# Layer normalisation of the first four tiles: tile 1's mean and variance by two ScalarE passes, doubled columns by GpSimd, V's parts and copies in another order

## The chip, the cores and the metric

The kernel runs on one core of a Trainium2 chip. The metric is the device time of one execution in microseconds. Engines are named as in the profile: PE is TensorE (matmuls; PEld its weight loads), DVE is VectorE, ACT is ScalarE, POOL is GpSimd, SP is SyncE, which here only issues transfers.

## The reference

The input x has 2048 rows of 576 columns in bfloat16. It is normalised without weights, and an attention over a sliding window and a gated feed-forward layer run side by side on the result:

```python
def _layernorm(x, axis=-1, eps=1e-5):
    m = jnp.mean(x, axis=axis, keepdims=True)
    v = jnp.var(x, axis=axis, keepdims=True)
    return (x - m) / jnp.sqrt(v + eps)
...
    xn = _layernorm(x, axis=-1)
    return x + _A_ref(xn, A_wqkv, A_wo) + _B_ref(xn, B_w1, B_w3, B_w2)
```

`_A_ref` projects xn to q, k and v (32 heads of 18 columns), lets each row see itself and the 255 rows before it, applies softmax and multiplies by wo. `_B_ref` computes (silu(xn @ w1) * (xn @ w3)) @ w2 with 4608 inner columns.

## The kernel before

The 2048 rows go in four chunks of 512, each of four tiles of 128 rows. For each chunk there are projections (line 439), 36 units of the feed-forward layer's first products (L675) with the attention's scores, exponentials and products dealt in between (L559, L568, L616), and then the sums of the second products and the output (L741, L760). Nearly all of it is TensorE's work, and the matmuls use half of the array's rows each (`tile_position`), so two run side by side.

Everything is recorded by `add(engine, ...)` in the order of the Python code. Each engine executes its own instructions strictly in that order; `_Prog.resolve` works out from the buffers' keys (r = reads, w = writes a new version, j = joins the writers of the present one) which semaphores an instruction has to wait for. So where a call stands in the code decides what it is queued behind.

The change is in the prologue, before the first chunk's projections. There the four tiles of chunk 0 are normalised and turned. (The tiles of the later chunks go another way, through a transposing DMA in `xn_send`.) For each tile t with buffers i = t % 2:

- `load_x` brings the tile into `xp`; tile 0 on SP's queue, tiles 1 to 3 on ScalarE's.
- `ln_stats` computes mean and variance on VectorE: a statistics instruction for each half of the columns (L355, L357), an aggregation into `mv` (L358). Then 1e-5 is added into `vpe` (L359, on VectorE for tiles 0 and 3, on GpSimd for 1 and 2), and GpSimd raises that to the power -0.5 into `rstd` (L361).
- `ln_apply` writes `xn` = (x - mean) * rstd on VectorE (L367). The row of `xn` is 640 wide: 576 columns, and then the last 64 once more, so that the fifth block of 128 holds columns 512 to 575 twice. It is done in two instructions, of 576 and of 64 columns.
- `xn_turn` transposes `xn` on TensorE by ten small matmuls with the identity into two banks of PSUM (L379), five blocks by two halves of the rows, and copies them to `xnT` (L390): for tiles 0 to 2 two ScalarE copies, for tile 3 one ScalarE and one VectorE copy. The banks are `SC` = (6, 7) for tiles 0 and 2 and `JOBS[1]` = (2, 3) for tiles 1 and 3.

V's projection (`proj_part` with kind "v") has ten matmuls in part 0 and eight in part 1 for each tile. `proj_begin` records part 0 of a new product and then part 1 of the one still open; `proj_end` records only that part 1 and the copies from PSUM to `va` (`v_evac`, L488 on ScalarE and L490 on VectorE, two instructions each). For tiles 0 and 1 these copies are held in the lists `moves` and `late` and recorded after the loop. V's tile 2 uses the banks `SC` again. `warm` issues matmuls on zeros.

Meanwhile GpSimd clears buffers and, when Q's and K's weights have landed, deals them into `wp` with nine copies (L851, `deal`); Q's and K's projections need them. SP issues the loads of x, V's weights and Q's and K's weights, then the first six parts of w13 (L315, behind tile 1's `xnT`), then the two copies `xn_swap` that fill `xnS` from `xnT` with the halves of the partitions exchanged (L404). In `unit_pairs` matmuls n = 4 to 7 read `xnS`, the others `xnT`.

Of the kernel before, what the change touches and what calls it, by code (L numbers as in the profile page):

```python
# [5 lines left out]
dt = mybir.dt  # L6
ACT = mybir.ActivationFunctionType
# [157 lines left out]
def bass_parallel_sum__sliding_block__glu_gated_swiglu__prompt_kernel(  # L165
# [13 lines left out]
    Dh = D // H  # L179
# [18 lines left out]
    with ExitStack() as es:  # L198
# [121 lines left out]
        def load_w13(behind=(), parts=6):  # L320
            for _ in range(parts):
                load_part((), behind)
# [26 lines left out]
                w=[("w2", s)], after=after, dma=f"w2_{s}")  # L349


        def ln_stats(t, s, part):
            i = t % 2
            if part == 0:
                add("dve", lambda e: e.bn_stats(stats[i][:, 0, :], xp[s][:, 0:HD]), r=[("xp", s)], w=[("stats", i)])  # L355
                return
            add("dve", lambda e: e.bn_stats(stats[i][:, 1, :], xp[s][:, HD:D]), r=[("xp", s)], j=[("stats", i)])  # L357
            add("dve", lambda e: e.bn_aggr(mv[i][:], stats[i][:]), r=[("stats", i)], w=[("mv", i)])  # L358
            add("dve" if t in (0, TB - 1) else "pool", lambda e: e.tensor_scalar(vpe[i][:], mv[i][:, 1:2], 1e-5, None, op0=ALU.add),  # L359
                r=[("mv", i)], w=[("vpe", i)])  # L360
            add("pool", lambda e: e.tensor_tensor(rstd[i][:], vpe[i][:], neghalf[:], ALU.pow),  # L361
                r=[("vpe", i), "neghalf"], w=[("rstd", i)])

        def ln_apply(t, s):
            i = t % 2
            for n, (c0, c1) in enumerate(((0, D), (512, D))):
                add("dve", lambda e, n=n, c0=c0, c1=c1: e.tensor_scalar(  # L367
                    xn[i][:, c0 + 64 * n:c1 + 64 * n], xp[s][:, c0:c1], mv[i][:, 0:1], rstd[i][:, 0:1],
                    op0=ALU.subtract, op1=ALU.mult),
                    r=[("xp", s), ("mv", i), ("rstd", i)], **{"j" if n else "w": [("xn", i)]})  # L370

        def xn_turn(t, banks, eng="dve"):
            i = t % 2
            c, tt = divmod(t, TB)
            for k in range(5):
                for r in range(2):
                    r0 = 64 * r
                    bv = half_bank(banks[r])[:, 64 * k:64 * k + 64]
                    add("pe", lambda e, bv=bv, r0=r0, k=k: e.transpose(  # L379
                        bv, xn[i][r0:r0 + 64, k * 128:(k + 1) * 128], ident[r0:r0 + 64, r0:r0 + 64],  # L380
                        tile_position=(r0, 0)),
                        r=[("xn", i), "ident"], **{"j" if k else "w": [("ps", banks[r])]})
            both = PS[:, banks[0]:banks[0] + 2, :].bitcast(dt.bfloat16)
            src = both[:, :, 0:320].rearrange("p r (k f) -> p k r f", f=64)
            dst = xnT[:, c % 2, :, tt * 128:(tt + 1) * 128].rearrange("p k (r f) -> p k r f", f=64)
            for n, (k0, k1) in enumerate(((0, 2), (2, 5))):
                d, s = dst[:, k0:k1, :, :], src[:, k0:k1, :, :]
                if eng[1] == "dve":
                    d, s = dst[:, :, n, :], src[:, :, n, :]
                move = (lambda e, d=d, s=s: e.tensor_copy(d, s)) if eng[n] == "dve" else (lambda e, d=d, s=s: e.activation(d, s, ACT.Copy))  # L390
                add(eng[n], move, r=[("ps", b) for b in banks],
                    **({"j": [("xnT", c % 2, tt)]} if n else {"w": [("xnT", c % 2, tt), ("xnTa", tt)]}))

        def xn_send(t):
            i = t % 2
            c, tt = divmod(t, TB)
            add("sp", lambda e: e.dma_start_transpose(
                xnT[:, c % 2, :, tt * 128:(tt + 1) * 128], xn[i][:]),
                r=[("xn", i)], w=[("xnT", c % 2, tt)], dma=f"xnT{tt}")

        def xn_swap(c, eng):
            for n in range(2):
# [5 lines left out]
        def xk(c):  # L408
            return [("xnT", c % 2, tt) for tt in range(TB)]
# [36 lines left out]
        def proj_out(c, what, banks, later=None, late=None):  # L446
            kind, i = what
            b = banks[0]
            if kind == "q":
                t0, t1 = pair_of(c, i)  # L450
                add("dve", lambda e: e.tensor_copy(stage[:, t0, :], PS[:, b, :]), r=[("ps", b)], w=st_keys(t0))
                add("act", lambda e: e.activation(stage[:, t1, :], PS[:, b + 1, :], ACT.Copy),  # L452
                    r=[("ps", b + 1)], w=st_keys(t1))
            elif kind == "8":
                add("dve", lambda e: e.tensor_copy(
                    stage[:, i, :].rearrange("p (b f) -> p b f", b=2), PS[:, b:b + 2, 0:CH // 2]),
                    r=[("ps", b), ("ps", b + 1)], w=st_keys(i))
            else:
                for r, (eng, held) in enumerate((("act", late), ("dve", later))):
                    move = lambda r=r, eng=eng: v_evac(c, i, b, r, eng)  # L460
                    move() if held is None else held.append(move)

        COST = {"q": 1.0, "8": 0.5, "v": 0.5625}
        PROJ = [("q", 0), ("q", 1), ("v", 0), ("q", 2), ("v", 1), ("q", 3), ("v", 2), ("8", 7), ("v", 3)]
# [9 lines left out]
        def proj_begin(c, what, banks=None):  # L474
            banks = banks or job()
            last = proj_part(c, what, banks, 0)
            got = proj_end()
            pend.append((c, what, banks, last))
            return got

        def v_evac(c, tt, b, r, eng):
            pos = (c * NB + 2 * tt + r) % NV
            for p in range(2):
                src = PS[64 * r:64 * r + 64, b:b + 2, 0:HD].rearrange("p b (n e d) -> p e b n d", e=2, d=Dh)[:, p, :, :, :]
                dst = va[64 * p:64 * p + 64, pos, :, :, 0:Dh].rearrange("p (b g) n d -> p b (g n) d", b=2)
                kw = {"j" if p else "w": [("va", pos)]}
                if eng == "act":
                    add("act", lambda e, dst=dst, src=src: e.activation(dst, src, ACT.Copy), r=[("ps", b), ("ps", b + 1)], **kw)  # L488
                else:
                    add("dve", lambda e, dst=dst, src=src: e.tensor_copy(dst, src), r=[("ps", b), ("ps", b + 1)], **kw)  # L490

        def keys_of(a, b, p0, n, p):
            return kv[p0:p0 + n, a:b, :, KB * p:KB * p + KB].rearrange("q g b f -> q (g b) f")
# [172 lines left out]
        def unit_pairs(c, u, n0, n1, b0):  # L666

            fc, fl = divmod(u, 4)
            sl, wt = w13_at(c * NFC + fc)
            for n in range(n0, n1):  # L670
                for r in range(2):
                    r0 = 64 * r
                    k = 8 if n == 8 else (2 * n + r if n < 4 else 2 * (n - 4) + 1 - r)
                    src = xnT[r0:r0 + 64, c % 2, k // 2, :] if n in (0, 1, 2, 3, 8) else xnS[r0:r0 + 64, n - 4, :]
                    op = add("pe", lambda e, n=n, r0=r0, r=r, k=k, src=src: e.matmul(  # L675
                        PS[:, b0 + r, :], wt[r0:r0 + 64, k, fl * 128:(fl + 1) * 128], src,
                        start=(n == 0), stop=(n == 8), tile_position=(r0, 0)),
                        r=[("w13", sl), "xnS"] + xk(c), **{"j" if n else "w": [("ps", b0 + r)]})
            return op

        def unit_tanh(u, b0):
# [111 lines left out]
        def warm(b, n):  # L793
            for k in range(n):
                add("pe", lambda e: e.matmul(PS[:, b, :], oq[:, 0:128], oq[:], start=True, stop=True),
                    r=["oq0"], **{"j" if k else "w": [("ps", b)]})
# [17 lines left out]
        def clear_keys(a, b, behind=()):  # L814
            add("pool", lambda e: e.memset(kv[:, a:b, :, :].bitcast(dt.float32), 0.0),
                r=list(behind), w=[("k", g) for g in range(a, b)])

        clear_keys(0, 2)
        for p in range(2):
            ln_stats(0, xslot[0], p)  # L820
        moves, late = [], []
        for i in range(TB):
            if i + 1 < TB:
                for p in range(2):
                    ln_stats(i + 1, xslot[i + 1], p)
            ln_apply(i, xslot[i])
            xn_turn(i, JOBS[1] if i % 2 else SC, ("act", "dve" if i + 1 == TB else "act"))
            if i == 0:
                warm(3, 1)
                proj_begin(0, ("v", 0))  # L830
            elif i == 1:
                load_w13([("xnT", 0, 1)])
                proj_end(moves, late)
                proj_begin(0, ("v", 1))
            elif i == 2:
                proj_end(moves, late)
        for move in moves + late:
            move()
        xn_swap(0, ("sp", "sp"))
        proj_begin(0, ("v", 2), SC)  # L840
        proj_begin(0, ("v", 3))
        wf = wa[:, :, :].bitcast(dt.float32).rearrange("p k (n g c) -> p k n g c", n=2, c=2 * Dh)
        wpf = wp[:, :, :, :].bitcast(dt.float32)
# [268 lines left out]
```

## Time and profile before

| what | value |
| --- | --- |
| median of 3 runs | 559.09 us (559.08 to 559.09) |
| the profiled execution's own time | 559.1 us |
| its span, first to last instruction | 557.4 us |
| granted TensorE clock | 1.00 |
| TensorE busy | 552.2 us, 99% of the span |
| VectorE, ScalarE, GpSimd busy | 56%, 45%, 29% |
| TensorE busy in 0 to 5 us / 5 to 10 us / 10 to 15 us | 3.76 / 3.77 / 4.93 us |

A row of the timeline gives start and length in us, engine, line, operation, what it writes and reads, shapes and how many instructions are drawn together; in brackets stands how long the engine was idle before it and what ended that. The chain that ended last is followed back from the last instruction to what released each. The end of a matmul in the trace is modelled, so that the starts are the better marks of its pace.

### The profile page before, as it was taken

What the parts mean: (1) busy time and instruction counts of PE and PEld (TensorE: products, weight loads), DVE (VectorE), ACT (ScalarE), POOL (GpSimd) and SP (SyncE); (2) the same over time, 40 slices, a digit from 0 to 9 for tenths busy, and PEclk for the clock granted to TensorE, in tenths of its full rate; (3) what the DMA queues carried; (4) which work ended last, traced back from release to release, by engine and by line L of the source; (5) the groups of instructions that cost most, each with busy time, mean ns of one, the idle gap of its engine ahead of it and who ended that gap; (6) DMA issues with size and microseconds to landing.
All of it is one profiled execution on the core that took longest, in us unless ns stands there. A gap on an engine that the chain in (4) does not pass through costs nothing.

```text
span 557.4 us, 18205 instructions
## 1 busy us (share of the span) xinstructions
PE 552.2 (99%) x8012; PEld 345.5 (62%) x8012; DVE 311.0 (56%) x586; ACT 252.9 (45%) x352; POOL 163.1 (29%) x384
## 2 busy tenths in 40 slices
PE   8999999999999999999999999999999999999998
PEld 4445455677687455477766545547777664555776
DVE  8566798710365778851056668884105567767211
ACT  4357776100287776600037777650005676676000
POOL 6413454400033445330003344533000333433000
PEclk9999999999999999999999999999999999999999
DMA  9998889777556657656846746566683674651650
GB/s 251 205 195 181 192 205 220 134 181 189 139 135 140 147 135 165 153 146 181 199 110 139 171 110 171 125 162 165 162 196 87 139 171 123 151 135 28 167 151 22
DMA packets 127893, 86.07 MB, mean 154 GB/s; under 512 B 35430, under 2 KB 125502, under 8 KB 127814
## 3 DMA queue, kind: packets, MB, share of 16 engines
q1 hardware_dynamic: 88994, 62.88, 48.8%
q10 hardware_dynamic: 38820, 22.02, 15.8%
q8 instruction: 63, 1.03, 0.9%
q14 instruction: 16, 0.13, 0.1%
HBM read 71.37 MB, written 2.36 MB: 132 GB/s over the span
## 4 chain that ended last, share of the span: by engine, by line
PE 98%; DVE 1%; DMA 0%; POOL 0%; issue 0%
PE ps L675 50%; PE ps L741 29%; PE ps L439 9%; PE ps L559 6%; PE ps L616 4%; DMA xp<-in_A_x_dram 0%; DVE xn L367 0%; DVE stats L355 0%; DVE stats L357 0%; DVE mv L358 0%; POOL rstd L361 0%; DVE ofin L760 0%; DVE vpe L359 0%; PE ps L379 0%
## 5 line engine op out<-in xcount | busy, mean ns | idle before, releaser
L675 PE MATMUL ps<-xnT,w 64*128 64x512 bf16 x1400 | 182.1, 376 | 0.0
L675 PE MATMUL ps<-xnS,w 64*128 64x512 bf16 x1120 | 155.1, 376 | 0.0
L741 PE MATMUL ps<-w,hT 64*128 64x288 bf16 x2288 | 143.7, 283 | 0.0
L690 DVE SCALAR_TENSOR_TENSOR gs<-th,ps 128x512 bf16<-128x512 bf16 x144 | 97.9, 680 | 80.3 <-ACT th L684 79.5
L568 ACT ACTIVATE pt<-ps 128x1024 bf16<-128x1024 f32 (+1 forms) x112 | 113.1, 1010 | 64.0 <-PE ps L559 62.9
L741 PEld LDWEIGHTS ps<-w,hT 64*128 64x128 bf16 x2288 | 111.7, 94 | 29.6 <-issue 0.4
L675 PEld LDWEIGHTS ps<-xnT,w 64*128 64x128 bf16 x1400 | 72.9, 94 | 55.9
L595 POOL TENSOR_TENSOR pt<-pt,mk 128x128 int32<-128x128 int32 (+1 forms) x199 | 80.3, 425 | 79.5 <-ACT pt L568 79.5
L693 DVE SCALAR_TENSOR_TENSOR hT<-gs,ps 128x512 bf16<-128x512 bf16 x144 | 98.9, 687 | 5.0
L684 ACT ACTIVATE th<-ps 128x512 bf16<-128x512 f32 x144 | 85.4, 593 | 23.5 <-PE ps L675 23.3
L675 PEld LDWEIGHTS ps<-xnS,w 64*128 64x128 bf16 x1120 | 59.4, 94 | 50.8
L760 DVE TENSOR_TENSOR ofin<-ps,xp 128x288 bf16<-128x288 f32 x32 | 12.7, 452 | 125.8 <-PE ps L741 125.8
L452 ACT ACTIVATE stage<-ps 128x512 bf16<-128x512 f32 x16 | 9.6, 597 | 143.6 <-PE ps L439 141.3
L595 POOL TENSOR_TENSOR hT<-hT,mk 128x128 int32<-128x128 int32 (+1 forms) x31 | 12.4, 420 | 170.5 <-ACT hT L568 170.5
L559 PE MATMUL ps<-qv,kv 64*128 64x320 bf16 (+4 forms) x528 | 53.6, 260 | 0.0
L559 PEld LDWEIGHTS ps<-qv,kv 64*128 64x128 bf16 x528 | 28.1, 94 | 24.9 <-ACT pt L568 0.5
L439 PE MATMUL ps<-xnT,wp 64*128 64x512 bf16 (+1 forms) x360 | 39.0, 355 | 0.0
L568 ACT ACTIVATE stage<-ps 128x1024 bf16<-128x1024 f32 x24 | 24.6, 1023 | 12.6 <-PE ps L559 12.6
L638 DVE STREAM_TRANSPOSE od<-oq 128x256 bf16<-128x256 bf16 x64 | 25.8, 428 | 6.3 <-POOL oq L631 6.3
L439 PEld LDWEIGHTS ps<-xnT,wp 64*128 64x128 bf16 x360 | 20.1, 94 | 13.0
L439 PE MATMUL ps<-wv,xnT 64*128 64x288 bf16 x288 | 22.0, 283 | 0.2 <-ACT xnT L390 0.2
L595 POOL TENSOR_TENSOR stage<-stage,mk 128x128 int32<-128x128 int32 (+1 forms) x42 | 17.0, 422 | 17.3 <-ACT stage L568 17.2
(59 smaller groups left out, 334.8 us busy)
## 6 DMA issues: line engine op xcount, KB each, us to landing
w<-in_B_w_dram SPq DMA_DIRECT2D x210, 192.0 KB, 4.1
w<-in_B_w_dram ACTq DMA_DIRECT2D x70, 288.0 KB, 3.6
xp<-in_A_x_dram SPq DMA_DIRECT2D x29, 144.0 KB, 3.4
out_dram<-ofin SPq DMA_DIRECT2D x32, 72.0 KB, 3.1
xnS<-xnT SPq DMA_DIRECT2D x8, 256.0 KB, 5.1
oT<-od SPq DMA_DIRECT2D x56, 36.0 KB
pt<-in_A_wqkv_dram SPq DMA_DIRECT2D x4, 288.0 KB, 5.6
hT<-in_B_w_dram SPq DMA_DIRECT2D x6, 192.0 KB, 7.4
```

The lines of the kernel that those rows point to most:

```text
L439: op = add("pe", lambda e, out_=out_, st=st, mv=mv, n=n, r0=r0, first=first: e.matmul(out_, st, mv, start=first, stop=(part == 1 and n == ...
L559: add("pe", lambda e, r0=r0, out_=out_, kb=kb, q0=q0, nb=nb: e.matmul(out_, kb4[r0:r0 + 64, g, kb + NV - NB, :] if kb < 0 else kv[r0:r0 + ...
L568: add("act", lambda e: e.activation(pt_slot(sl)[:, 0:w, :], PS[:, SC[0]:SC[1] + 1, 0:w].rearrange("p r q -> p q r"), ACT.Exp, scale=scale) ...
L595: add("pool", lambda e, vb=vb, mm=mm: e.tensor_tensor(vb, vb, mm, ALU.mult), r=(key if n == 0 else []) + ["mk"], **{"w" if n == 0 else "j" ...
L616: add("pe", lambda e, p=p, q=q, pr=pr, sl=sl, g=g, pos=pos, q0=q0, nb=nb, col=col, first=first, n=n: e.matmul(PS[32 * q:32 * q + VW, banks ...
L638: add("dve", lambda e: e.transpose(od[i][:, g % 2, c0:c0 + CH // 2], oq[:, c0:c0 + CH // 2]), r=["oq", "oq0"], **{"j" if half or g % 2 els ...
L675: op = add("pe", lambda e, n=n, r0=r0, r=r, k=k, src=src: e.matmul(PS[:, b0 + r, :], wt[r0:r0 + 64, k, fl * 128:(fl + 1) * 128], src, star ...
L684: add("act", lambda e: e.activation(th[i][:], PS[:, bg, :], ACT.Tanh, scale=0.5), r=[("ps", bg)], w=[("th", i)])
L690: add("dve", lambda e: e.scalar_tensor_tensor(out=gs[i][:], in0=th[i][:], scalar=1.0, in1=PS[:, bg, :], op0=ALU.add, op1=ALU.mult), r=[("t ...
L693: add("dve", lambda e: e.scalar_tensor_tensor(out=hT[:, u, :], in0=gs[i][:], scalar=0.5, in1=PS[:, bu, :], op0=ALU.mult, op1=ALU.mult), r= ...
L741: op = add("pe", lambda e: e.matmul(PS[:, bank, 0:HD], stat, move, start=new, stop=False, skip_group_check=True, **tile), r=keys, after=he ...
L760: add("dve", lambda e: e.tensor_tensor(ofin[:, o, :], PS[:, bank, 0:HD], xp[xs[n]][:, d0:d0 + HD], ALU.add), r=[("ps", bank), ("xp", xs[n] ...
```

## The change

- Tile 1's mean and variance come from ScalarE (`ln_stats_act`): one pass over the tile copies it scaled by -1/(576*24) and sums the row into `vpe`, which is minus the mean over 24; a second pass squares x/24 plus that and sums the row into `mv`, which is the variance. What they write besides is left in a part of `hT` that is free at that time. GpSimd multiplies `vpe` by -24 to get the mean, adds 1e-5 and takes the power. Before, VectorE's three instructions and GpSimd's addition and power did this.
- The addition of 1e-5 and the power are taken out into `ln_root`. In the prologue the addition is on VectorE for tiles 0, 2 and 3 (tile 2's was on GpSimd), and the power is recorded where the order now wants it.
- For tiles 0 to 3 `ln_apply` writes columns 0 to 511 on VectorE and the doubled block of 128 columns on GpSimd in one instruction that reads the 64 columns twice. The doubled block has a key of its own, `xnd`, and only the last two of the ten transposes wait for it.
- The prologue's loop is written out by hand. VectorE's statistics of tile 2 begin before tile 0 is applied. On TensorE part 0 of V's tile 2 moves ahead of tile 3's turn, and part 1 of it directly behind that turn.
- The copies of V are recorded one instruction at a time. The first ScalarE and the first VectorE copy of tile 0 are recorded between tile 3's transposes and the copies from PSUM of that turn.
- In `unit_pairs` only the matmuls n = 4 to 7 wait for `xnS`, and only the others for `xnT`.

TensorE's order up to the first projection of Q was: turn 0, V0 part 0, turn 1, V0 part 1, V1 part 0, turn 2, V1 part 1, turn 3, V2 part 0, V3 part 0, V2 part 1. It becomes: turn 0, V0 part 0, turn 1, V0 part 1, V1 part 0, turn 2, V1 part 1, V2 part 0, turn 3, V2 part 1, V3 part 0.

```diff
+        def ln_root(t, eng=None):
+            i = t % 2
+            if eng is not None:
+                add(eng, lambda e: e.tensor_scalar(vpe[i][:], mv[i][:, 1:2], 1e-5, None, op0=ALU.add),
+                    r=[("mv", i)], w=[("vpe", i)])
+                return
+            add("pool", lambda e: e.tensor_tensor(rstd[i][:], vpe[i][:], neghalf[:], ALU.pow),
+                r=[("vpe", i), "neghalf"], w=[("rstd", i)])
+
+        def ln_stats_act(t, s):
+            i = t % 2
+            junk = hT[:, 0:3, :].rearrange("p t c -> p (t c)").bitcast(dt.float32)[:, 0:D]
+            keys = [("h", n) for n in range(3)]
+            root = float(D) ** 0.5
+            add("act", lambda e: e.activation(junk, xp[s][:], ACT.Copy, scale=-1.0 / (D * root), accum_out=vpe[i][:]),
+                r=[("xp", s)], w=[("vpe", i), *keys])
+            add("act", lambda e: e.activation(junk, xp[s][:], ACT.Square, bias=vpe[i][:], scale=1.0 / root, accum_out=mv[i][:, 1:2]),
+                r=[("xp", s), ("vpe", i)], w=[("mv", i), *keys])
+            add("pool", lambda e: e.tensor_scalar(mv[i][:, 0:1], vpe[i][:], -root, None, op0=ALU.mult),
+                r=[("vpe", i)], j=[("mv", i)])
+            ln_root(t, "pool")
+            ln_root(t)
...
         def ln_apply(t, s):
             i = t % 2
-            for n, (c0, c1) in enumerate(((0, D), (512, D))):
-                add("dve", lambda e, n=n, c0=c0, c1=c1: e.tensor_scalar(
-                    xn[i][:, c0 + 64 * n:c1 + 64 * n], xp[s][:, c0:c1], mv[i][:, 0:1], rstd[i][:, 0:1],
-                    op0=ALU.subtract, op1=ALU.mult),
-                    r=[("xp", s), ("mv", i), ("rstd", i)], **{"j" if n else "w": [("xn", i)]})
+            parts = [("dve", 0, 512, 0), ("pool", 512, D, 1)] if t < TB else [("dve", 0, D, 0), ("dve", 512, D, 2)]
+            for eng, c0, c1, n in parts:
+                src = xp[s][:, c0:c1]
+                if n == 1:
+                    dst, src = xn[i][:, 512:640].rearrange("p (a c) -> p a c", a=2), src.unsqueeze(1).to_broadcast([128, 2, 64])
+                else:
+                    dst = xn[i][:, c0 + 32 * n:c1 + 32 * n]
+                add(eng, lambda e, dst=dst, src=src: e.tensor_scalar(
+                    dst, src, mv[i][:, 0:1], rstd[i][:, 0:1], op0=ALU.subtract, op1=ALU.mult),
+                    r=[("xp", s), ("mv", i), ("rstd", i)], w=[("xnd", i) if n else ("xn", i)])
...
-                        r=[("xn", i), "ident"], **{"j" if k else "w": [("ps", banks[r])]})
+                        r=[("xn" if k < 4 else "xnd", i), "ident"], **{"j" if k else "w": [("ps", banks[r])]})
+            for what in between:
+                what()
...
-                        r=[("w13", sl), "xnS"] + xk(c), **{"j" if n else "w": [("ps", b0 + r)]})
+                        r=[("w13", sl)] + (["xnS"] if 4 <= n < 8 else xk(c)), **{"j" if n else "w": [("ps", b0 + r)]})
...
+        moves, late = [], []
         for p in range(2):
             ln_stats(0, xslot[0], p)
-        moves, late = [], []
-        for i in range(TB):
-            if i + 1 < TB:
-                for p in range(2):
-                    ln_stats(i + 1, xslot[i + 1], p)
-            ln_apply(i, xslot[i])
-            xn_turn(i, JOBS[1] if i % 2 else SC, ("act", "dve" if i + 1 == TB else "act"))
-            if i == 0:
-                warm(3, 1)
-                proj_begin(0, ("v", 0))
-            elif i == 1:
-                load_w13([("xnT", 0, 1)])
-                proj_end(moves, late)
-                proj_begin(0, ("v", 1))
-            elif i == 2:
-                proj_end(moves, late)
+        ln_root(0, "dve")
+        ln_root(0)
+        ln_stats(2, xslot[2], 0)
+        ln_apply(0, xslot[0])
+        ln_stats_act(1, xslot[1])
+        xn_turn(0, SC, ("act", "act"))
+        warm(3, 1)
+        proj_begin(0, ("v", 0))
+        ln_stats(2, xslot[2], 1)
+        ln_root(2, "dve")
+        ln_stats(3, xslot[3], 0)
+        ln_apply(1, xslot[1])
+        ln_root(2)
+        xn_turn(1, JOBS[1], ("act", "act"))
+        load_w13([("xnT", 0, 1)])
+        proj_end(moves, late)
+        proj_begin(0, ("v", 1))
+        ln_stats(3, xslot[3], 1)
+        ln_root(3, "dve")
+        ln_apply(2, xslot[2])
+        ln_root(3)
+        xn_turn(2, SC, ("act", "act"))
+        ln_apply(3, xslot[3])
+        first = [moves.pop(0), late.pop(0)]
+        proj_end(moves, late)
+        proj_begin(0, ("v", 2), SC)
+        xn_turn(3, JOBS[1], ("act", "dve"), first)
         for move in moves + late:
             move()
         xn_swap(0, ("sp", "sp"))
-        proj_begin(0, ("v", 2), SC)
+        proj_end()
         proj_begin(0, ("v", 3))
```

More of the change, by code (lines that the diff above doesn't have):

```diff
@@ L358, in ln_stats, with xn_turn @@
             add("dve", lambda e: e.bn_aggr(mv[i][:], stats[i][:]), r=[("stats", i)], w=[("mv", i)])
[L359 to L362, printed above, removed]
+            if t >= TB:
+                ln_root(t, "pool")
+                ln_root(t)
         def ln_apply(t, s):
             i = t % 2
-            for n, (c0, c1) in enumerate(((0, D), (512, D))):
-                add("dve", lambda e, n=n, c0=c0, c1=c1: e.tensor_scalar(
-                    xn[i][:, c0 + 64 * n:c1 + 64 * n], xp[s][:, c0:c1], mv[i][:, 0:1], rstd[i][:, 0:1],
-                    op0=ALU.subtract, op1=ALU.mult),
-                    r=[("xp", s), ("mv", i), ("rstd", i)], **{"j" if n else "w": [("xn", i)]})
-        def xn_turn(t, banks, eng="dve"):
+            parts = [("dve", 0, 512, 0), ("pool", 512, D, 1)] if t < TB else [("dve", 0, D, 0), ("dve", 512, D, 2)]
[8 more added lines that the diff above has]
+                    r=[("xp", s), ("mv", i), ("rstd", i)], w=[("xnd", i) if n else ("xn", i)])
+        def xn_turn(t, banks, eng, between=()):
             i = t % 2
@@ L398, in xn_send @@
                 xnT[:, c % 2, :, tt * 128:(tt + 1) * 128], xn[i][:]),
-                r=[("xn", i)], w=[("xnT", c % 2, tt)], dma=f"xnT{tt}")
+                r=[("xn", i), ("xnd", i)], w=[("xnT", c % 2, tt)], dma=f"xnT{tt}")
         def xn_swap(c, eng):
@@ L459, in proj_out @@
                 for r, (eng, held) in enumerate((("act", late), ("dve", later))):
-                    move = lambda r=r, eng=eng: v_evac(c, i, b, r, eng)
-                    move() if held is None else held.append(move)
+                    for p in range(2):
+                        move = lambda r=r, eng=eng, p=p: v_evac(c, i, b, r, eng, p)
+                        move() if held is None else held.append(move)
         COST = {"q": 1.0, "8": 0.5, "v": 0.5625}
@@ L479, in proj_begin, with v_evac @@
             return got
-        def v_evac(c, tt, b, r, eng):
+        def v_evac(c, tt, b, r, eng, p):
             pos = (c * NB + 2 * tt + r) % NV
-            for p in range(2):
[L484 to L490, printed above, removed]
+            src = PS[64 * r:64 * r + 64, b:b + 2, 0:HD].rearrange("p b (n e d) -> p e b n d", e=2, d=Dh)[:, p, :, :, :]
+            dst = va[64 * p:64 * p + 64, pos, :, :, 0:Dh].rearrange("p (b g) n d -> p b (g n) d", b=2)
+            kw = {"j" if p else "w": [("va", pos)]}
+            if eng == "act":
+                add("act", lambda e, dst=dst, src=src: e.activation(dst, src, ACT.Copy), r=[("ps", b), ("ps", b + 1)], **kw)
+            else:
+                add("dve", lambda e, dst=dst, src=src: e.tensor_copy(dst, src), r=[("ps", b), ("ps", b + 1)], **kw)
         def keys_of(a, b, p0, n, p):
@@ L818, in bass_parallel_sum__sliding_block__glu_gated_swiglu__prompt_kernel @@
         clear_keys(0, 2)
+        moves, late = [], []
         for p in range(2):
             ln_stats(0, xslot[0], p)
-        moves, late = [], []
-        for i in range(TB):
-            if i + 1 < TB:
-                for p in range(2):
-                    ln_stats(i + 1, xslot[i + 1], p)
-            ln_apply(i, xslot[i])
-            xn_turn(i, JOBS[1] if i % 2 else SC, ("act", "dve" if i + 1 == TB else "act"))
-            if i == 0:
-                warm(3, 1)
-                proj_begin(0, ("v", 0))
-            elif i == 1:
-                load_w13([("xnT", 0, 1)])
-                proj_end(moves, late)
-                proj_begin(0, ("v", 1))
-            elif i == 2:
-                proj_end(moves, late)
+        ln_root(0, "dve")
[25 more added lines that the diff above has]
+        xn_turn(3, JOBS[1], ("act", "dve"), first)
         for move in moves + late:
```

## The prediction

> **What bounds the kernel now.** I read the page first (busy shares, the chain that ended last), then the chain in order of time, then the timeline of the first 13 us, single instructions of it last.
>
> ```profile
> PE 552.2 (99%) x8012; PEld 345.5 (62%) x8012; DVE 311.0 (56%) x586; ACT 252.9 (45%) x352; POOL 163.1 (29%) x384
> ...
> PE 98%; DVE 1%; DMA 0%; POOL 0%; issue 0%
> ```
>
> ```profile
> 10.70 11.12 PE ps L439 x126
> 21.82 12.95 PE ps L675 x120
> ```
>
> TensorE is the bound, and from 10.70 us on it never waits for data: 126 projection matmuls run into the first units. Listing the starts of all later matmuls, I find no distance over 0.31 us after 12 us. So the end of the span moves one for one with the moment at which TensorE enters its gapless stretch. I take as marker the first projection of Q, "Q0" (the ten matmuls of 512 columns at 12.41). Only what comes before it can be won or lost.
>
> ```profile
> 4.85 0.55 POOL L361 TENSOR_TENSOR rstd<-vpe,neghalf 128x1 f32<-128x1 f32 x1 [1.06 <-DVE vpe L359]
> ...
> 5.65 0.59 DVE L367 TENSOR_SCALAR xn<-xp,mv,rstd 128x576 bf16<-128x576 bf16 x2
> ...
> 6.30 0.32 PE L379 MATMUL ps<-ident,xn 64*128 64x64 bf16 x10 [0.98 <-DVE xn L367]
> ...
> 7.86 0.31 PE L379 MATMUL ps<-ident,xn 64*128 64x64 bf16 x10
> ...
> 9.50 0.32 PE L379 MATMUL ps<-ident,xn 64*128 64x64 bf16 x10
> ...
> 9.87 1.31 ACT L390 ACTIVATE xnT<-ps 128x256 bf16<-128x256 bf16 x3 [0.89 <-PE ps L379]
> ...
> 10.25 3.67 POOL L851 COPY wp<-pt 128x45 f32<-128x45 f32 x9 [0.61 <-DMA pt<-in_A_wqkv_dram]
> ...
> 10.38 0.32 PE L379 MATMUL ps<-ident,xn 64*128 64x64 bf16 x10
> ...
> 12.41 1.24 PE L439 MATMUL ps<-xnT,wp 64*128 64x512 bf16 x10
> ```
>
> The four L379 rows are the turns of the four tiles, T0 to T3. Between them stand V's products in halves (V0a is the first ten matmuls of tile 0, V0b the last eight). Order before: T0, V0a, T1, V0b, V1a, T2, V1b, T3, V2a, V3a, V2b, Q0. T0 waits for VectorE, which is busy with tile 1's statistics until 5.74 though rstd is there at 5.40; T2 and T3 wait for VectorE too (9.45 and 10.32, plus 0.06).
>
> **The change, step by step.** A handover costs 0.06 (VectorE to TensorE, 6.24 to 6.30), 0.04 (GpSimd to VectorE, TensorE to ScalarE), 0.08 (GpSimd to itself, 6.11 to 6.19).
>
> *T0.* VectorE loses tile 1's statistics here and does one half of tile 2's (landed 5.05, 0.45 us), to 5.53. The apply, now of 512 columns, took 0.29 behind a busy engine for 576; I take 0.28, so 5.81, and T0 starts at 5.87 instead of 6.30.
>
> *The doubled columns.* The 64 columns twice, 0.21 us of VectorE per tile, become one GpSimd tensor_scalar of 128x128, g, which no row shows. Nearest below: an affine_select of 128x128, 0.29. Above: the mask product of 128x128, two inputs, 0.42 to 0.46; far above: 128x288 products, 0.68. I take 0.42, the same tile size on the same engine. But both halves wait for the same rstd, so they meet:
>
> ```profile
> 76.19 0.91 DVE L367 TENSOR_SCALAR xn<-xp,mv,rstd 128x576 bf16<-128x576 bf16 x2
> 76.36 0.71 POOL L631 TENSOR_TENSOR oq<-ofin,rden 128x288 bf16<-128x288 f32 x1 [1.50 <-DVE rden L630]
> ```
>
> The same pair of applies that takes 0.59 in the prologue takes 0.91 here, and ends 0.04 after GpSimd's product. The other way round, the vpe addition on GpSimd at 5.82 takes 0.29 instead of 0.22 and ends 0.08 after the apply it met; so 0.14 of it lies ahead of the block. I therefore count one as standing still for the other. VectorE is released first (0.04 against 0.08): xnd0 can only work from 5.81 and ends at 5.81 + 0.42 - 0.14 = 6.09.
>
> The Trainium skill, SBUF — State Buffer, section Who interferes with whom, says that VectorE in a two-port mode, which a tensor_scalar can enter, and GpSimd take one shared port pair as an exclusive lock, so that the second blocks fully. The trace agrees (0.91 against 0.59); by that rule the sum is the one below, without it that of the first rival.
>
> *Tile 1's statistics.* ScalarE starts when its table (3.56) and tile 1 (3.68) are there. Its copies take 0.38 for 256 and 0.49 for 384 columns, so 0.80 ns a column and 0.18 fixed: 0.64 for 576, two passes and a handover to about 5.04. Accumulator and bias vector are priced by no row (from nothing to double, 6.3); they are used only by the addition at 6.38, so I count nothing. GpSimd then does, behind xnd0: mean (0.22, starting 0.06 before xnd0 ends, as the copies of L851 follow one another), addition (0.08 + 0.05 for two semaphores, as the first L851 copy shows, + 0.22), power (0.08 + 0.57): rstd1 at 6.09 - 0.06 + 0.22 + 0.13 + 0.22 + 0.65 = 7.25. Before it was there at 6.77, and VectorE took it up at 7.12. Queued behind these on GpSimd are xnd1 and rstd2; T1 waits for them.
>
> *T1.* The apply from an idle engine took 0.43; 0.04 + 0.41 gives 7.70. xnd1 stands until then and ends at 7.98. Eight transposes run from 7.76, the last pair waits to 8.04 instead of 7.88. T1 is thus worth a start at 7.92, against 7.86 before: the early T0 (V0a would be done at 7.42) is lost on GpSimd's chain.
>
> *T1 to T2.* ScalarE's two evacuations and V1a between them, 7.86 to 9.40, are unchanged: 1.55. T2 may start at 9.47; GpSimd and VectorE have tile 2 ready by then (rstd2 8.49, xnd2 9.22). Before: 9.50.
>
> *T2 to Q0, the new order* T2, V1b, V2a, T3, V2b, V3a, Q0. V2a writes the banks of T2 and so waits for both evacuations: 9.50 to 10.69 before, 1.18; before, T3 filled part of that, now only V1b (0.49) does. V2a 0.62. T3 to V3a: 0.36 to the evacuation's start, 0.44, 0.06 = 0.86, of which V2b covers some 0.7; before, V2a behind T3 hid it whole. V3a 0.61. So 1.18 + 0.62 + 0.86 + 0.61 = 3.27 against 12.41 - 9.50 = 2.91 before. Q0 at 9.47 + 3.27 = 12.74: **0.33 later**.
>
> *At nothing.* V0's first pieces ahead of T3's evacuation (VectorE 0.46, ScalarE 0.40): apply 3 is done near 10.18, so they end by 10.7, before that evacuation at 11.6; without this cover up to 0.46. V0's second pieces now stand behind it and end near 12.47; Q0 needs their banks, cover 0.27. GpSimd's deals (L851) start when xnd3 is done, 10.46 instead of 10.25; Q0 needs three of them, 1.0 us, so 11.46. SP's first w13 load waits for T1's evacuation (0.06 later); the xnS copies behind its six issues wait at 13.1 as before, landed by 20.85, first needed at 22.52. That unit_pairs no longer waits for xnS in its outer matmuls takes away a wait that had ended by the 21.65 at which unit 0 starts. The later chunks keep instructions and order.
>
> **Sum.** Profiled execution: 559.10 (span 557.4, 1.7 around it); median 559.09, the same. 559.09 + 0.33 = 559.4. In general the block makes it 0.33 + 2(g - 0.42), since g enters at xnd0 and at xnd1. About what a measurement of this kernel can tell from no change is 0.2%, 1.12 us, so this is within it.
>
> **Rivals.**
> 1. *No block, a short g.* xnd0 5.90, rstd1 7.06, T1 7.57: 0.35 earlier than above, so -0.02; with g at 0.29, -0.15; 558.9 to 559.1. V0a's end at 7.42 is the floor, -0.17. For it: the meetings above are with longer GpSimd products. Against it: 0.91 against 0.59.
> 2. *GpSimd becomes the bound: slower.* g with two scalar vectors per partition could cost far more than a product; chain xnd0, mean, addition, power, xnd1 stands ahead of T1. It decides (over 0.2%) from g = 0.82 on; at 1.0 it gives +1.49, 560.6. For: one-element pow takes 0.57, a one-element addition 0.22, so GpSimd's cost hangs on the kind of operation. Against: selects, copies and products of this size lie at 0.29 to 0.46.
> 3. *ScalarE's passes come late.* They decide from 1.3 us a pass on; at 1.9 they end at 7.6 and rstd1 comes 1.2 later: near 560.6. Against: every ScalarE row is linear in columns, and no second table load is in the program.
>
> To win more than 0.2%, Q0 would have to start at 11.29; T1 at its floor gives 12.24.
>
> **Numbers.** Forecast 0.50 (its own range 559.2 to 559.7, g from 0.35 to 0.55); rival 1 0.30; rival 2 0.09; rival 3 0.03; what I don't see 0.05 within 0.2% and 0.03 faster. Faster 0.03, same 0.85, slower 0.12. The range goes from rival 1's floor, 558.9, to g = 0.69 with a power that meets an apply (0.69 instead of 0.57, as at 8.95): +0.87 + 0.12, 560.1.
>
> **What would show it.** T0 near 5.9; the GpSimd tensor_scalar at 0.42 or its end 0.28 behind the apply's; rstd1 near 7.25; T1's last pair late; two gaps on TensorE, before V2a (0.5) and V3a (0.15); Q0 at 12.7. Wrong if Q0 starts before 12.2 or after 13.5, or if TensorE waits later than Q0.

## The result, and the profile after

The changed kernel takes 560.25 us (median; 560.00 to 561.87), the kernel before 559.14 us in the same comparison. The ratio is 1.002, 95% interval 1.0012 to 1.0027: slower by 1.1 us, and outside the forecast range (558.9 to 560.1). The profiled execution took 560.29 us with a span of 558.6 us, against 559.10 and 557.4.

The page of the changed kernel, TensorE's busy time and the engines of the chain that ended last; then that chain in order of time (start and length in us):

```profile
PE 553.0 (99%) x8012; PEld 345.4 (62%) x8012; DVE 309.7 (55%) x580; ACT 254.5 (46%) x356; POOL 166.4 (30%) x388
...
PE 98%; POOL 1%; DMA 0%; DVE 0%; issue 0%; ACT 0%; POOLq 0%
```

```profile
5.47 0.94 POOL xn L395
7.88 0.96 POOL xn L395
...
12.46 10.56 PE ps L468 x116
23.02 12.95 PE ps L704 x120
```

The 1% that was VectorE's is now GpSimd's: two of its doubled blocks, 0.94 and 0.96 us long, stand in the chain itself, with its small instructions between them. The timeline shows how they got there (L395 is the apply, on DVE and on POOL; L358 the power; L406 the transposes; L468 the projections):

```profile
5.47 0.94 POOL L395 TENSOR_SCALAR xn<-xp,mv,rstd 128x128 bf16<-128x128 bf16 x1
5.49 0.46 DVE L378 BATCH_NORM_STATS2 stats<-xp 128x6 f32<-128x288 bf16 x1 [0.77 <-DMA xp<-in_A_x_dram]
5.87 0.40 DVE L395 TENSOR_SCALAR xn<-xp,mv,rstd 128x512 bf16<-128x512 bf16 x1
...
6.33 0.34 PE L406 MATMUL ps<-ident,xn 64*128 64x64 bf16 x10 [0.63 <-DVE xn L395]
6.49 0.25 POOL L370 TENSOR_SCALAR mv<-vpe 128x1 f32<-128x1 f32 x1
...
7.20 0.57 POOL L358 TENSOR_TENSOR rstd<-vpe,neghalf 128x1 f32<-128x1 f32 x1
...
7.81 0.41 DVE L395 TENSOR_SCALAR xn<-xp,mv,rstd 128x512 bf16<-128x512 bf16 x1 [0.37 <-POOL rstd L358]
7.88 0.95 POOL L395 TENSOR_SCALAR xn<-xp,mv,rstd 128x128 bf16<-128x128 bf16 x1
...
8.88 0.20 PE L406 MATMUL ps<-ident,xn 64*128 64x64 bf16 x2 [0.32 <-POOL xn L395]
...
10.33 0.34 PE L406 MATMUL ps<-ident,xn 64*128 64x64 bf16 x10
...
13.62 1.24 PE L468 MATMUL ps<-xnT,wp 64*128 64x512 bf16 x10
```

Tile 1's power in the kernel before, in the same view:

```profile
6.19 0.57 POOL L361 TENSOR_TENSOR rstd<-vpe,neghalf 128x1 f32<-128x1 f32 x1
```

Tile 0's block keeps GpSimd until 6.41. Only then come tile 1's mean (6.49), addition (6.90) and power (7.20, done at 7.77, where before rstd of tile 1 was there at 6.77). Then tile 1's own block runs to 8.83, and T1's last pair starts at 8.88; before, all of T1 was issued by 7.98. Q0 starts at 13.62 instead of 12.41, 1.21 us later, and the span has grown by 1.2. Nothing is won or lost after Q0.

### The profile page after: what moved, and what is told of

Its sections match the earlier page's. It is cut to its first block, busy times and chain, and to the rows that moved or that the text cites. A ratio compares the mean times of both kernels' runs of the same rounds, so it can differ in the third digit from the quotient of the medians.

```text
span 558.6 us, 18212 instructions
## 1 busy us (share of the span) xinstructions
PE 553.0 (99%) x8012; PEld 345.4 (62%) x8012; DVE 309.7 (55%) x580; ACT 254.5 (46%) x356; POOL 166.4 (30%) x388
## 4 chain that ended last, share of the span: by engine, by line
PE 98%; POOL 1%; DMA 0%; DVE 0%; issue 0%; ACT 0%; POOLq 0%
PE ps L704 50%; PE ps L770 29%; PE ps L468 9%; PE ps L588 6%; PE ps L645 4%; DMA xp<-in_A_x_dram 0%; POOL xn L395 0%; POOL rstd L358 0%; ACT xnT L419 0%; PE ps L406 0%; DVE stats L378 0%; DVE ofin L789 0%; DVE stats L380 0%; POOL mv L370 0%; POOL vpe L355 0%
## 5 line engine op out<-in xcount | busy, mean ns | idle before, releaser
L468 PE MATMUL ps<-xnT,wp 64*128 64x512 bf16 (+1 forms) x360 | 39.0, 355 | 0.0
L468 PEld LDWEIGHTS ps<-xnT,wp 64*128 64x128 bf16 x360 | 20.1, 94 | 13.0
L468 PE MATMUL ps<-wv,xnT 64*128 64x288 bf16 x288 | 22.4, 283 | 0.6 <-ACT xnT L419 0.6
```

Source lines behind the costliest of these rows:

```text
L468: op = add("pe", lambda e, out_=out_, st=st, mv=mv, n=n, r0=r0, first=first: e.matmul(out_, st, mv, start=first, stop=(part == 1 and n == ...
```

## The experiments

Theory: GpSimd's instruction costs twice what the forecast gave it and stands twice in the chain to T1. Rivals: the new order and ScalarE's passes carry the loss; or VectorE's apply, which each block meets, stretches a short instruction.

**The doubled block back on VectorE**, all else as changed:

```diff
-            parts = [("dve", 0, 512, 0), ("pool", 512, D, 1)] if t < TB else ...
+            parts = [("dve", 0, 512, 0), ("dve", 512, D, 1)] if t < TB else ...
```

> The changed kernel, with the doubled block of the first four tiles written by VectorE again (the same instruction, another engine). Theory A, GpSimd's tensor_scalar is the cause: without it GpSimd's chain is rstd0 at 5.36, mean, addition, power, rstd1 near 6.75, and VectorE's order sets tile 1's turn: T1 near 7.8 to 8.2 (by whether tile 2 lands at 5.05 or 5.47) instead of a last pair at 8.88, so Q0 at T1 + 4.82 = 12.6 to 13.0 instead of 13.62; about 0.6 to 1.0 us faster than the changed kernel, 0.2 to 0.6 slower than the kernel before. Theory B, the new order and the ScalarE passes carry the loss: Q0 stays near 13.5 and the time at 560.2.

559.64 us against 559.15, ratio 1.0007 (0.9998 to 1.0016). TensorE's rows:

```profile
7.70 0.43 PE L406 MATMUL ps<-ident,xn 64*128 64x64 bf16 x10
...
12.63 1.24 PE L468 MATMUL ps<-xnT,wp 64*128 64x512 bf16 x10
```

T1 is whole at 7.70 and Q0 moves from 13.62 to 12.63, as the theory expects: between these two profiled executions, 0.99 us of the 1.21 go with the engine of this one instruction. By medians it is 0.6 of 1.1, and that is the safer figure: this profile caught one of the fastest executions of the kernel (559.29), with tile 2's load landed at 5.05 instead of 5.47.

**The block on GpSimd alone**, in the kernel before:

```diff
-            for n, (c0, c1) in enumerate(((0, D), (512, D))):
+            parts = [("dve", 0, 512, 0), ("pool", 512, D, 1)] if t < TB else ...
...
-                        r=[("xn", i), "ident"], ...
+                        r=[("xn" if k < 4 else "xnd", i), "ident"], ...
```

> The kernel before, with only the doubled block of the first four tiles on GpSimd. Theory A: with 0.94 us each, xnd0 ends at 6.41, rstd1 comes at 7.24, xnd1 ends at 8.25, xnd2 near 10.1, xnd3 near 11.6, and T3 waits for that: V2a near 11.7, Q0 near 13.5, 1.1 us slower than the kernel before. Theory B (order and passes carry the loss): the block hides behind V's products, Q0 within 0.2 us of 12.41.

561.60 us, ratio 1.0041 (1.0028 to 1.0053): slower by 2.45, twice what was expected. Timeline:

```profile
5.91 0.29 PE L384 MATMUL ps<-ident,xn 64*128 64x64 bf16 x8 [0.78 <-DVE xn L373]
...
7.47 0.23 PE L384 MATMUL ps<-ident,xn 64*128 64x64 bf16 x2 [1.27 <-POOL xn L373]
...
8.28 1.38 PE L444 MATMUL ps<-wv,xnT 64*128 64x288 bf16 x10
...
10.79 1.58 POOL L373 TENSOR_SCALAR xn<-xp,mv,rstd 128x128 bf16<-128x128 bf16 x2
10.82 0.55 DVE L373 TENSOR_SCALAR xn<-xp,mv,rstd 128x512 bf16<-128x512 bf16 x1 [0.44 <-POOL rstd L361]
...
14.44 0.81 PE L444 MATMUL ps<-xnT,wp 64*128 64x512 bf16 x6
```

Two things were missing from the expectation. In the old order tile 1's addition and power are recorded ahead of tile 0's block, which therefore starts at 6.59 and not at 5.5. And V0a takes 1.38 instead of 0.83: TensorE runs at half pace after its waits. Windows of this run (start and end; length; busy time of PE, PEld, DVE, ACT and POOL, with their instructions; then the mean granted clock, here 0.60, 0.54 and 1.00; share and GB/s of the DMA engines):

```profile
7.00:9.00 2.00, 1.50 (x11) 0.69 (x13) 1.22 (x4) 0.77 (x2) 1.51 (x4) 0.60 1.13 261
9.00:11.00 2.00, 2.00 (x29) 1.52 (x27) 0.86 (x4) 0.77 (x2) 1.41 (x3) 0.54 1.13 279
11.00:13.00 2.00, 1.91 (x44) 1.40 (x40) 0.70 (x2) 1.10 (x3) 2.00 (x5) 1.00 0.42 120
```

**Another form of the instruction in each tile**, in the changed kernel:

```diff
+                m0, m1 = (0.0, 1.0) if t == 1 and n == 1 else (mv[i][:, 0:1], rstd[i][:, 0:1])
+                if t == 2 and n == 1:
+                    dst, src = xn[i][:, 512:640], xp[s][:, 448:576]
...
+                parts = [("dve", 0, 512, 0), ("dve", 512, D, 2), ("pool", 512, D, 0.5)]    # t == 3
```

> The changed kernel with another form of GpSimd's instruction in each tile: tile 0 as it is; tile 1 with the constants 0 and 1 in place of mean and rstd (so these 64 columns of tile 1 stay unnormalised); tile 2 from 128 columns in one stretch (448 to 575) instead of 64 read twice, so that half of that block holds other columns; tile 3 with 64 columns, the other 64 written by VectorE. If the two scalar vectors cost the time: tile 1 drops from 0.94 to some 0.35 to 0.45 and the others stay. If reading the columns twice does: tile 2 drops to 0.45. If it is per column: tile 3 drops to some 0.55. If VectorE's apply holds GpSimd up (the port theory of the prediction): all four stay above 0.8, for all four meet an apply.

559.94 us, one execution. The blocks took 0.82, 0.67 (constants), 0.93 (one stretch) and 0.71 (64 columns). Reading the columns twice costs nothing. Each of the others takes a part and none the whole. All four met an apply, but tile 0's, 0.19 after its start, cost it nothing: 0.82 here against 0.94 in the changed kernel, where the apply came 0.40 after it. So the run doesn't separate the instruction's own cost from that of the meeting. The next two do.

**The block behind the apply**, so that the two never run at once:

```diff
-                    r=[("xp", s), ("mv", i), ("rstd", i)], w=...
+                    r=[("xp", s), ("mv", i), ("rstd", i)] + ([("xn", i)] if n == 1 else []), w=...
```

> The changed kernel, with GpSimd's doubled block of each tile waiting for VectorE's apply of that tile, so that the two never run at once. If the instruction costs 0.8 by itself and the apply adds the rest: about 0.80 in all four tiles instead of 0.93 to 0.95. If the apply it meets makes up most of it (the port theory): 0.42 to 0.55. If the apply has no part in it: 0.94. In each case the chain to T1's last pair grows by the wait, about 0.4 per tile less what an instruction saves, so Q0 between 13.6 and 14.4.

GpSimd's rows of the timeline:

```profile
6.31 0.81 POOL L395 TENSOR_SCALAR xn<-xp,mv,rstd 128x128 bf16<-128x128 bf16 x1 [0.98 <-DVE xn L395]
...
9.04 0.82 POOL L395 TENSOR_SCALAR xn<-xp,mv,rstd 128x128 bf16<-128x128 bf16 x1 [0.56 <-DVE xn L395]
...
12.84 0.80 POOL L395 TENSOR_SCALAR xn<-xp,mv,rstd 128x128 bf16<-128x128 bf16 x1 [0.56 <-DVE xn L395]
```

So 0.81 is the instruction's own, and meeting the apply adds 0.12 to 0.14 in the changed kernel. (Not at every meeting: tile 0 of the run before this one lost nothing, and what decides it stays open.) The rival that made the apply the main cause falls. 562.06 us; Q0 came at 15.53, later than the 14.4 expected, again with a stretch at half clock.

**Forms, behind the apply**:

```diff
+                m0, m1 = (0.0, 1.0) if t == 0 and n == 1 else (mv[i][:, 0:1], rstd[i][:, 0:1])
+                two = dict(op0=ALU.subtract, op1=ALU.mult)
+                if t == 2 and n == 1:
+                    m0, m1, two = rstd[i][:, 0:1], None, dict(op0=ALU.mult)
...
+                parts = [("dve", 0, 512, 0), ("dve", 512, D, 2), ("pool", 512, D, 0.5)]    # t == 1
```

> As the run before, with another form of GpSimd's instruction in each tile: tile 0 with the constants 0 and 1 instead of mean and rstd (these columns of tile 0 stay unnormalised); tile 1 with 64 columns (the other 64 by VectorE); tile 2 with one operation and one vector (times rstd; the mean is not subtracted there); tile 3 as it is. If the vectors cost, tiles 0 and 2 lie below tile 3, by about 0.07 for each vector (0.67 against 0.82 to 0.93 under an apply); if the columns cost, tile 1 lies some 0.2 below tile 3; if the second operation costs, tile 2 lies below tile 0.

```profile
6.44 0.67 POOL L403 TENSOR_SCALAR xn<-xp 128x128 bf16<-128x128 bf16 x1 [1.09 <-DVE xn L403]
...
9.02 0.61 POOL L403 TENSOR_SCALAR xn<-xp,mv,rstd 128x64 bf16<-128x64 bf16 x1 [0.56 <-DVE xn L403]
...
10.72 0.62 POOL L403 TENSOR_SCALAR xn<-xp,rstd 128x128 bf16<-128x128 bf16 x1 [0.56 <-DVE xn L403]
...
12.43 0.80 POOL L403 TENSOR_SCALAR xn<-xp,mv,rstd 128x128 bf16<-128x128 bf16 x1 [0.55 <-DVE xn L403]
```

Against 0.80: 64 columns fewer save 0.19, so about 3 ns a column; two vectors cost 0.13, so 0.07 each; the second operation costs what is left between tile 2 (0.62, one vector) and tile 0 with a vector more (0.67 + 0.07 = 0.74), 0.12. 128 columns at 3 ns are 0.38, and about as much does not depend on the columns. (562.21 us.)

**The order alone**, in the kernel before:

```diff
             elif i == 2:
                 proj_end(moves, late)
+                proj_begin(0, ("v", 2), SC)
...
-        proj_begin(0, ("v", 2), SC)
+        proj_end()
```

> The kernel before, with only V2a moved ahead of T3 and V2b behind it. Both theories price this step apart: by the prediction's working T2 to Q0 grows from 2.91 to 3.27, so Q0 at 12.77 and 0.36 us slower. A rival reading, that T3 was late for VectorE anyway (10.38) and so the order costs nothing, gives Q0 at 12.41 and no difference.

559.68 us against 559.15, ratio 1.0011 (1.0002 to 1.002). Timeline:

```profile
9.54 0.32 PE L379 MATMUL ps<-ident,xn 64*128 64x64 bf16 x10
...
12.05 3.34 DVE L490 CAST va<-ps 64x288 bf16<-64x288 f32 x7
...
13.08 1.25 PE L439 MATMUL ps<-xnT,wp 64*128 64x512 bf16 x10
```

T2 to Q0 takes 3.54 where the forecast said 3.27. V3a starts at 12.18 and would be done at 12.8; but V0's copies now run behind T3's evacuation, VectorE's two from 12.05 to 12.99 (ScalarE's two end by 12.86), and Q0 needs the banks that they empty.

**The order with V0's first copies moved too**, on top of the last edit, with `between` and the single copies as in the change:

```diff
-            xn_turn(i, JOBS[1] if i % 2 else SC, ("act", "dve" if i + 1 == TB else "act"))
+            xn_turn(i, JOBS[1] if i % 2 else SC, ("act", "dve" if i + 1 == TB else "act"),
+                    [moves.pop(0), late.pop(0)] if i + 1 == TB else ())
```

> The kernel before, with V2a ahead of T3, V2b behind it, and V0's first ScalarE and VectorE copies ahead of T3's evacuation: the whole third part of the change alone. If V0's late copies (banks 4 and 5) were what held Q0 at 13.08 in the run with the order alone, T2 to Q0 is now the 3.27 of the prediction instead of 3.54: Q0 near 12.8, 0.35 slower than the kernel before. If the copies have no part, 3.54 again and 0.6 slower.

559.46 us against 559.12, 0.34 more by medians; the ratio, 1.0003 (0.9994 to 1.0012), doesn't tell it from no difference. The timeline does:

```profile
9.66 0.32 PE L379 MATMUL ps<-ident,xn 64*128 64x64 bf16 x10
...
12.93 1.24 PE L441 MATMUL ps<-xnT,wp 64*128 64x512 bf16 x10
```

T2 to Q0 is 3.27, the forecast's figure, against 2.91 in the kernel before. So moving those copies mends a wait that the new order itself makes, and the order costs the 0.36.

**The ScalarE passes alone**, in the kernel before:

```diff
-            if i + 1 < TB:
+            if i == 0:
+                ln_stats_act(1, xslot[1])
+            elif i + 1 < TB:
```

> The kernel before, with only tile 1's mean and variance by the two ScalarE passes (mean, addition and power on GpSimd). By the prediction's rows the passes are done before GpSimd asks for them, so VectorE applies tile 0 at once (T0 at 6.1), T1 follows V0a at 7.6 to 7.7 and T2 at 9.25; Q0 near 12.2, about 0.2 us faster than the kernel before. A rival: the passes or the longer chain on GpSimd (mean, addition, power) make rstd1 later than 7.1, T1 later than 7.86 and the kernel slower; another: the weights of Q and K land late and hide the gain.

558.96 us against 559.04, ratio 0.9998 (0.9989 to 1.0006): no difference that can be told. T1 came at 7.74 and T2 at 9.29, both close to what was expected, and Q0 could have followed V's products at 12.20; it started at 12.36:

```profile
10.47 1.89 PE L462 MATMUL ps<-wv,xnT 64*128 64x288 bf16 x28
11.30 1.78 POOL L876 COPY wp<-pt 128x45 f32<-128x45 f32 x5 [1.89 <-DMA pt<-in_A_wqkv_dram]
12.35 0.76 PEld L462 LDWEIGHTS ps<-xnT,wp 64*128 64x128 bf16 x10 [0.31 <-POOL wp L876]
12.36 1.25 PE L462 MATMUL ps<-xnT,wp 64*128 64x512 bf16 x10
```

Here Q's and K's weights landed so late that the deals began at 11.30 instead of 10.25, and Q0 waited for the third of them (12.30). That was the last of the rivals named for this run. So the passes lose nothing, and in this execution what they win ends at these weights.

**The change without its two losing parts**: the block on VectorE, T3 again ahead of V2a with V's copies all behind it, tile 1 applied ahead of tile 3's statistics.

```diff
...
-        ln_stats(3, xslot[3], 0)
         ln_apply(1, xslot[1])
+        ln_stats(3, xslot[3], 0)
...
-        proj_begin(0, ("v", 2), SC)
-        xn_turn(3, JOBS[1], ("act", "dve"), first)
+        xn_turn(3, JOBS[1], ("act", "dve"))
```

> The changed kernel with the doubled block on VectorE, tile 1 applied ahead of tile 3's statistics, and T3 again ahead of V2a as in the kernel before (V's copies all behind T3's evacuation). If GpSimd's instruction (0.6 to 1.0 us, by the first run) and the order (0.36) are what the change loses, this is what is left of it: T1 near 7.7, T2 near 9.4, V2a near 10.5, Q0 near 12.2 to 12.3, about 0.15 faster than the kernel before. If the ScalarE passes lose time too, it stays slower than the kernel before.

559.02 us against 559.04, ratio 1.0002 (0.9993 to 1.0012). In the profiled execution Q0 starts at 12.20, 0.21 before that of the kernel before, and the span is 557.0; over all executions no gain can be told. By medians the run with only the block on VectorE was 0.49 above the kernel before, and this one is level with it. The order alone has 0.34 of that; the rest, some 0.15, no run prices by itself.

**T3 ahead of V2a, with the block on GpSimd**, all else as changed:

```diff
-        proj_begin(0, ("v", 2), SC)
         xn_turn(3, JOBS[1], ("act", "dve"), first)
...
-        proj_end()
+        proj_begin(0, ("v", 2), SC)
```

> The changed kernel, with T3 again ahead of V2a (all else as changed, doubled block on GpSimd). If the new order costs 0.36 whatever stands before it, Q0 at 13.26 instead of 13.62. If the order pays where tile 3 is late (its block on GpSimd ends at 11.96): V2a has to wait for T3, near 12.15, V3a near 13.38 to 12.95, Q0 near 13.8, 0.2 slower than the changed kernel.

560.55 us against 559.12, ratio 1.0021 (1.0012 to 1.003), which overlaps that of the changed kernel. Its profiled execution had TensorE at half clock for a while (Q0 at 14.13), so the trace can't decide either. It is not faster by the 0.36 that the order costs elsewhere. By medians it is 0.3 above the changed kernel (1.43 against 1.11 over the kernel before), as the second reading has it, but that lies within the intervals; whether the order pays where tile 3 is late stays open.

**TensorE kept busy in its waits**, on top of the block behind the apply:

```diff
             for k in range(5):
+                if k == 4 and t < 2:
+                    warm(0 if t else 3, 4)
```

> The run with GpSimd's block behind the apply (Q0 at 15.53, V's products at a distance of 0.24 instead of 0.12 per pair between 9.96 and 13.1, clock 0.997), with four matmuls on zeros put in T0's and in T1's wait for the block. If the halved pace comes from TensorE standing idle just before: pairs at 0.12 again, clock 1.000, Q0 near 14.4 although TensorE does eight matmuls more. If it has another cause: 0.24 as before and Q0 at 15.5 or later.

561.89 us, one execution, clock 1.000. V's pairs stand 0.12 apart throughout, and Q0 comes at 15.22 instead of 15.53 although TensorE does eight more matmuls. So in this pair of single executions the halved pace goes with standing idle; but most of it had been hidden behind the waits for GpSimd, and the gain is 0.3, not 1.1.

## Why the prediction was wrong, step by step

- *Bound and marker*: right. Q0 moved by 1.21, the span by 1.2.
- *T0 at 5.87*: measured 6.33. VectorE now asks for tile 2's load before it applies tile 0, and that load landed at 5.47 here, not 5.05; in the runs where VectorE stood waiting for it, these statistics began between 5.08 and 5.74. It cost nothing only because T1 came later for another reason: that is luck.
- *g = 0.42*: this is the step that failed. Measured 0.93 to 0.95 in the changed kernel, 0.81 alone. Taking the mask product because tile and engine were the same was wrong: on GpSimd columns, vectors and operations each have a price. The high rival named this mechanism, gave its turning point (0.82) and had a chance of 0.09; the range stopped at g = 0.69.
- *The sum's form* held: 0.33 + 2(g - 0.42) gives 1.11 for the instruction's own 0.81, with the meeting already in the formula; measured 1.21. T1's last pair was put at 8.04 and came at 8.88. That it comes so close is partly luck, for two errors cancel: from the end of tile 0's block to tile 1's rstd the forecast has 1.16 and 1.36 passed (the mean started 0.08 after the block's end, not 0.06 before it), while each meeting was given 0.19 to 0.23 and cost 0.13 to 0.14.
- *The block by the apply*: too strong. In the changed kernel the apply takes its usual 0.41 and GpSimd loses 0.12 to 0.14; once, in the run with four forms, neither lost anything. In the run with the block alone GpSimd began at 10.79 and kept its 0.80, and the apply, 0.03 behind it, took 0.55 and was done at 11.37, before GpSimd was (11.59). The Trainium skill (SBUF — State Buffer, Who interferes with whom) says that when VectorE is in a two-port mode, whichever of it and GpSimd comes second stands fully until the first is done; none of these meetings shows that, other than the prediction's one with a GpSimd product at 76.36, and no run shows the mode.
- *ScalarE's passes at nothing*: right. They ended at 5.31 (forecast 5.04), first wanted at 6.5.
- *T2 to Q0, 3.27*: right, 3.29 in the changed kernel and 3.27 alone. *V0's first copies at nothing, cover 0.9*: right in place, and without the move they cost 0.27.

## What to carry to other kernels

Before work goes to GpSimd, price the very form of the instruction, with its columns, vectors and operations, and not another instruction of the same tile: here the wrong row was off by a factor of two, and the chain counted it twice. An instruction handed to another engine is queued in that engine's order too; here it stood ahead of the three small instructions for which the next tile was waiting. And where the working shows a term that enters twice and that no row prices, the range has to reach to where that term decides.

## What the runs showed of the hardware

- TensorE fell to half clock in the prologue in runs that made it stand idle there. In the run with the block alone, after waits of 0.78 and 1.27 us, matmul pairs ran 0.24 apart and the granted clock was 0.50 from 7.42 to 10.83, 3.4 us; all five timed executions of that kernel had a mean clock of 0.997. The changed kernel with waits of 0.63 and 0.32 kept 1.00 in the profile, but its slowest execution, 561.87, had 0.997. How much idling is enough was not measured. The Trainium skill (TensorE: Matmul & The Clock Gate, Part 1) has a gate that goes between half and full rate by the activity in a window of about 3.4 us; the stretch at half pace and the run with added matmuls agree with it.
- A ScalarE pass that sums into an accumulator is two instructions: 0.68 us for 576 columns, and a read of the accumulator of 0.19, of which 0.09 lies under the pass. The second pass, which squares and takes its bias from a vector, takes 0.78. The Trainium skill (ScalarE: Activation LUTs, What ACT_TABLE_LOAD costs) puts a vector operand at 0.09; the difference of the two passes agrees, though they also differ in their function and no run changes the vector alone.
